# Attention with a soft mixture of experts: second-layer weights in two-row units, weight loads begun later, merged first loads, last group's exponentials by pairs of heads

## The chip, the cores and the metric

One core of one Trainium2 chip runs the kernel. The metric is the device time in microseconds (us). Engines: PE (TensorE), PEld (its weight load), ACT (ScalarE), DVE (VectorE), POOL (GpSimd), SP (SyncE, which here only issues transfers); 16 DMA engines move data between the chip's memory (DRAM here) and the on-chip buffers.

## The reference, cut to what matters

```python
# q, k, v: (8 batches, 12 heads, 448 tokens, 64); cap = 30
s = cap * tanh(q @ k.T / 8 / cap)                 # per batch and head
attn = softmax(s) ; x = attn @ v                  # -> x: 3584 tokens x 768
logits = x @ phi                                  # phi: 768 x 32 (8 experts, 4 slots each)
slot_input = softmax(logits, over tokens).T @ x   # 32 x 768
h = relu(slot_input[e] @ w1[e])                   # w1: 8 x 768 x 1024
slot_out[e] = h @ w2[e]                           # w2: 8 x 1024 x 768
out = softmax(logits, over slots) @ slot_out      # 3584 x 768
```

All inputs and outputs are float32. The kernel computes in bf16 and fp16 with float32 sums.

## The kernel before, in words

**Groups.** The attention is cut into 24 groups of four heads (two pairs of heads, numbered 0 and 1). A group has 14 key tiles (`TILES`, L31): tiles 0 to 6 belong to pair 0, 7 to 13 to pair 1, of 128 keys each; of every seven, one is a "mixed" tile that holds the last 64 keys of both heads. The scores of a group come in six chunks (`CHUNKS`, L34) of 3, 2, 2, 2, 3, 2 tiles: PE computes them (L520, L523), ACT takes the tanh of a chunk at a time out of PSUM (L533). Then ACT takes the exponentials of the first nine tiles in one instruction (L541, 128x9x448). For the other five tiles DVE builds the exponentials as a sum of four terms (L548, `PH` 0 to 3). In the last group these are four tiles, and the fourteenth is a small exponential on ACT of its own (L541, 128x448). PE multiplies by the values (L558): `a0`, `a1` for pair 0; `d` (two tiles), `c0` to `c3` (the four terms) and, in the last group, `e` for pair 1. DVE divides by the sums (L591, L592), PE turns the result (L603), DVE copies it (L607), and the logits and slot sums follow.

**The order of the work.** A planner (`Plan`, from L68) lists all steps of the 24 groups with durations from a table (`COST`, L63) and due times shifted by two more tables (`DUE`, `HOLD`, L50 and L58), and picks the order in which they are written; each step is written by its entry in `EMIT` (L722). Each engine runs its instructions in that order, so a step that waits holds up everything behind it on its engine.

**Transfers.** The POOL queue carries the q loads (L406), the w1 weights in 24 parts of 512 KB (L341) and the w2 weights in 32 parts (L345) of 384 KB, all cast from float32 to bf16 on their way; POOL also casts V (L431). There is no room on chip for all of w2 during the attention: five parts stay in a buffer `w2b`, 27 are written to DRAM as bf16 (`w2d`) and read back by SP at the end (L874, `w2t`). SP issues the K loads (`kraw`, L411; DVE casts them, L417), the V loads (L423, four DMAs a group) and the stores of the output (L945, L963). The planner starts the weight parts at 3000 of its nanoseconds and spreads them up to the end of the attention, with the intervals of w1 and w2 parts as 4 to 3.

**First loads.** `load_first` (L440 to 454) fetches q and k of group 0 as float32: q0, k0 (pair 0), k1, q1 (pair 1), each into a 128x448 piece of `raw`. Each of the four is issued as two DMAs of 64 partitions, 112 KB each; k0 goes by the ACT queue, the rest by SP. Casts (L463), turns (L470) and copies (L477) of pair 0 are written out by hand (L750 to 761); those of pair 1 (`CA`, `T0`, `C0`) are steps of the planner. Memsets of the V buffers follow at L762 to 770.

**The end.** After the last group come the logits, slot sums and the first expert layer (L895), relu (L906, L909), a turn of the hidden values (`h_transp`, L911), and the second layer in two passes (L928): pass 0 gives columns 0 to 383 of the slot outputs, pass 1 columns 384 to 767. Each pass goes through all 64 blocks of 128 hidden units. A w2 part before is four blocks by one half of the columns, so pass 0 reads only half-0 parts; the reads from DRAM (L872) are sorted by half. A cast of half 0 (L985, L986) starts the output products and their stores, which run beside pass 1.

Of the kernel before, what the change touches and what calls it, by code (L numbers as in the profile page):

```python
# [10 lines left out]
BF16 = mybir.dt.bfloat16  # L11
# [6 lines left out]
P = 128  # L18
# [22 lines left out]
ND_LAST = 4  # L41
FULL, ROWS, COLS, QUARTERS = range(4)
# [7 lines left out]
DUE = {"C0k": 58662, "C0q": -424707, "CAk": -62736, "CAq": 128660, "CE": -181216, "CS": 121512, "CW": -420874,  # L50
# [7 lines left out]
HOLD = {"C0k": 102, "C0q": 1186, "CAk": 1500, "CAq": 919, "CE": 125, "CS": 183, "CX": 1447, "Ck": 546, "Cq": 841,  # L58
# [4 lines left out]
COST = dict(quad=9250, lat=200, dma=6000, form=95, sc=100, scm=200, act=0.833, act0=70, ts=242, ts0=90,  # L63
            pvf=31, turn=420, kturn=450, xturn=400, copy=540, kcopy=600, norm=780, vcast=1060, vscale=340, kcast=570, kdiag=300,
            issue=800, load=1400, part1=3200, part2=2450, same=300, page=6000)


class Plan:  # L68
# [5 lines left out]
    def op(self, name, eng, dur, deps=(), due=0.0, take=None, give=None, after=0.0, form=(FULL, FULL), port=False, mm=0):  # L74
        key = name[0] + (str(name[2]) if name[0] in ("PV", "NR", "PH", "EX", "LG", "SS") else "") + \
            (name[1] if name[0] in ("L", "X", "T", "C", "CA", "T0", "C0") else "")
        self.ops[name] = dict(name=name, eng=eng, dur=dur, deps=list(deps), due=due + DUE.get(key, 0.0),
                              key=key, hold=max(0, HOLD.get(key, 0)), take=take, give=give, after=after, form=form, port=port, mm=mm)

    def build(self):  # L80
# [11 lines left out]
        for Q in range(1, NQ):  # L92
            for n, nm in enumerate("kq"):
                t0 = Q * T - (2600, 1800)[n]
                if nm == "k":
                    op(("LK", Q), "SP", 400, [("KC", Q - 2)], t0 - 1.5 * T)
                    op(("XK", Q), "DMV", C["load"], [("LK", Q)], t0 - 1.5 * T)
                    op(("KC", Q), "DVE", C["kcast"], [("XK", Q), ("T", nm, Q - 1)], t0 - 0.5 * T, port=True)
                else:
                    op(("L", nm, Q), "POOL", C["issue"], [("T", nm, Q - 2)], t0 - 1.3 * T)  # L100
                    op(("X", nm, Q), "DMA", C["load"], [("L", nm, Q)], t0 - 1.3 * T)
# [4 lines left out]
        for Q in range(NQ):  # L106
            b, t0, lastq = Q // NQB, Q * T, Q == NQ - 1
            for s in range(nc):
# [21 lines left out]
            op(("EX", Q, 0), "ACT", C["act0"] + C["act"] * S * na, [("TH", Q, sa)],  # L130
               t0 + T * (first[sa] + CHUNKS[sa] + 2.5) / NQT)
            if ne:
                op(("EX", Q, 1), "ACT", C["act0"] + C["act"] * S * ne, [("TH", Q, nc - 1)], t0 + 2 * T)
            for i in range(PH):
# [4 lines left out]
                if i < PH - 1 and k >= 0:  # L139
                    deps.append(("PV", k // (PH - 1), f"c{k % (PH - 1)}"))  # L140
                op(("PH", Q, i), "DVE", C["ts0"] + C["ts"] * ((nd + 1) // 2), deps, t0 + T + 1100 * i, port=True)
            te = t0 + .8 * T
            vs = [("VC", Q), ("VS", Q)]
            op(("PV", Q, "a0"), "PE", 24 * C["pvf"], [("EX", Q, 0)] + vs, te, take=True, mm=24)
            op(("PV", Q, "a1"), "PE", 8 * C["pvf"], [("PV", Q, "a0")], te + 1, mm=8)
            op(("NR", Q, 0), "DVE", C["norm"], [("PV", Q, "a1"), ("SS", (Q - 4) // NQB, 1)], te + 1000,
               give=("PV", Q, "a0"))
            td = t0 + T + 1200
            op(("PV", Q, "d"), "PE", (8 + 4 * (NA - 8)) * C["pvf"], [("EX", Q, 0)] + vs, td - 10, take=True, mm=8 + 4 * (NA - 8))
            for i in range(PH):  # L150
                op(("PV", Q, f"c{i}"), "PE", 4 * nd * C["pvf"],
                   [("PH", Q, i), ("PV", Q, f"c{i - 1}" if i else "d")], td + 1100 * i, mm=4 * nd)
            if ne:
                op(("PV", Q, "e"), "PE", 4 * C["pvf"] * ne, [("EX", Q, 1), ("PV", Q, "c0")], td + 2500, mm=4 * ne)
            op(("NR", Q, 1), "DVE", C["norm"], [("PV", Q, "e"), ("PV", Q, f"c{PH - 1}"), ("SS", (Q - 4) // NQB, 1)],
               td + 5000, give=("PV", Q, "d"))
# [104 lines left out]
def kernel(  # L261
# [62 lines left out]
    w2b = wts.tile([P, KEPT, 4, HD], BF16, name="w2b")  # L324

    blocks = [(i, ft, gg) for i in range(E // 4) for ft in range(NFT) for gg in range(4)]

    def w2_src(n0, n):

        i, ft, gg = blocks[n0]  # L330
        return bass.AP(tensor=moe_w2.tensor,
                       offset=((4 * i + gg) * F + ft * P) * D,
                       ap=[[D, P], [F * D, n], [1, D]])
# [9 lines left out]
    def load_half(dst, n0, half):  # L343
        src = w2_src(n0, 4)
# [720 lines left out]
```

## Time and profile before

| what | value |
|---|---|
| time, median of 3 runs | 292.15 us (292.04 to 292.38) |
| profiled execution's own time | 294.73 us |
| its span, first to last instruction | 292.8 us |
| busy PE / ACT / DVE / POOL | 253.5 / 242.3 / 212.5 / 99.0 us |
| chain that ended last | ACT 38%, PE 31%, DMA 12%, DVE 10% |
| mean granted TensorE clock | 0.938 |
| moved by DMA | 75.30 MB in 59071 packets |

How to read it: the attention fills the span from about 11 to 240 us. ACT works without a break there, apart from the first 48 us, so a wait of ACT inside the attention lengthens the run. Before it come the first loads, behind it the two expert layers and the stores. The profiled execution took 294.73 us, 1.93 more than its span and 2.58 more than the median of the three runs.

### The profile page before, as it was taken

Reading aid. Unit: us, or ns where it says so; the run is one execution under the profiler, and the core shown is the slowest. Engines: PE = TensorE matmul, PEld = TensorE weight load, DVE = VectorE, ACT = ScalarE, POOL = GpSimd, SP = SyncE. Lnnn points to the kernel's source line nnn. Section 1 sums busy time; section 2 is a strip of 40 time slices with the busy share of each in tenths; the row PEclk is TensorE's granted clock in tenths of the full one; section 3 lists DMA queues with packets and bytes.
Section 4 is the critical chain, followed back from the end, with each engine's and each line's share of the span. In section 5 each row is a group of like instructions: output and inputs, shape, how many; then the busy total and the mean of one; then the engine's idle time right before and its main releaser. Section 6 shows DMA issues by size and latency. Waiting matters only on the chain.

```text
span 292.8 us, 10788 instructions
## 1 busy us (share of the span) xinstructions
PE 253.5 (87%) x4697; PEld 177.4 (61%) x4697; DVE 212.5 (73%) x407; ACT 242.3 (83%) x214; POOL 99.0 (34%) x165
## 2 busy tenths in 40 slices
PE   4799949989999999899999989999999879997700
PEld 4366645767766767667767776677676668543300
DVE  2548936878987898798988878987988764248720
ACT  0799957999999999999999999999999981236710
POOL 4463513512462424353446333553335200200000
PEclk9559986999999999999999999999999989999965
DMA  7999999999999999999999999999999999958995
GB/s 136 247 221 253 233 260 257 239 202 199 245 256 229 244 254 250 250 244 244 234 244 249 225 245 226 248 247 228 182 212 319 260 334 405 396 190 328 412 411 227
DMA packets 59071, 75.30 MB, mean 257 GB/s; under 512 B 4880, under 2 KB 48016, under 8 KB 59024
## 3 DMA queue, kind: packets, MB, share of 16 engines
q0 software_dynamic: 30464, 30.50, 63.4%
q1 hardware_dynamic: 28400, 43.89, 45.7%
q8 instruction: 37, 0.61, 0.8%
q10 hardware_dynamic: 160, 0.23, 0.3%
q14 instruction: 10, 0.08, 0.1%
HBM read 94.08 MB, written 21.63 MB: 395 GB/s over the span
## 4 chain that ended last, share of the span: by engine, by line
ACT 38%; PE 31%; DMA 12%; DVE 10%; issue 4%; SPq 1%; DVEq 0%; POOL 0%; ACTq 0%
ACT exa L541 18%; PE pv L558 12%; ACT exd L533 11%; ACT exa L533 8%; PE sc L523 6%; DMA kraw<-in_k_dram 5%; DMA vraw<-in_v_dram 3%; DVE term L548 3%; PE xps L603 2%; DMA raw<-in_q_dram 2%; DMA out_dram<-ob 2%; PE so_ps L928 2%; PE hp L895 2%; PE qps L494 2%; PE sc L520 2%
## 5 line engine op out<-in xcount | busy, mean ns | idle before, releaser
L533 ACT ACTIVATE exa<-sc 128x1344 f16<-128x1344 f32 (+1 forms) x96 | 91.7, 1036 | 5.7 <-PE sc L523 5.3
L541 ACT ACTIVATE exa<-exa 128x4032 bf16<-128x4032 f16 x24 | 86.0, 3585 | 0.0
L548 DVE TENSOR_SCALAR term<-exd 128x2240 uint16<-128x2240 f16 (+1 forms) x72 | 62.6, 892 | 1.6 <-PE pv L558 1.6
L523 PE MATMUL sc<-qT,kT 64*128 64x448 bf16 x288 | 58.0, 372 | 0.8 <-ACT exa L533 0.3
L558 PEld LDWEIGHTS <-term 128*128 128x128 bf16 x1428 | 48.6, 98 | 9.6 <-issue 6.8
L558 PE MATMUL pv<-vb,exa 128*128 128x65 bf16 x1056 | 46.0, 197 | 8.9 <-ACT exa L541 8.1
L558 PEld LDWEIGHTS <-exa 128*128 128x128 bf16 x1056 | 38.6, 100 | 21.7 <-ACT exa L541 10.4
L533 ACT ACTIVATE exd<-sc 128x1344 f16<-128x1344 f32 (+1 forms) x48 | 50.8, 1118 | 0.5 <-DVE xq L592 0.5
L406 POOL DMA_DIRECT2D qb<-in_q_dram x23 | 16.7, 726 | 73.5 <-PE qps L494 60.0
L558 PE MATMUL pv<-vb,term 128*128 128x65 bf16 x952 | 36.8, 195 | 0.0
L592 DVE TENSOR_TENSOR xq<-pv,rec 128x448 bf16<-128x448 f32 (+2 forms) x49 | 30.1, 615 | 3.1
L523 PEld LDWEIGHTS <-kT 64*128 64x128 bf16 x288 | 15.3, 93 | 19.5 <-issue 13.0
L431 POOL CAST vb<-vraw 128x1024 bf16<-128x1024 f32 x24 | 25.5, 1062 | 1.3 <-DMA vraw<-in_v_dram 0.7
L607 DVE COPY xT<-xps 128x896 bf16<-128x896 bf16 x23 | 14.3, 624 | 11.2 <-PE xps L603 11.1
L345 POOL DMA_DIRECT2D w2d<-in_moe_w_dram x27 | 21.1, 799 | 0.8 <-issue 0.8
L548 DVE TENSOR_SCALAR exd<-exd 128x2240 uint16<-128x2240 f16 (+1 forms) x24 | 20.3, 848 | 0.8
L499 DVE COPY kT<-kps 128x1024 bf16<-128x1024 bf16 x23 | 15.8, 688 | 5.1 <-PE kps L490 4.8
L430 POOL COPY seen<-xq 1x1 bf16<-1x1 bf16 x22 | 4.3, 197 | 43.9 <-DVE xq L592 43.9
L558 PE MATMUL pv<-vw,exd 128*128 128x65 bf16 x476 | 18.6, 193 | 0.6
L558 PE MATMUL pv<-vw,term 128*128 128x65 bf16 x476 | 18.6, 193 | 0.3 <-DVE term L548 0.2
L591 DVE RECIPROCAL rec<-pv 128x7 f32<-128x7 f32 (+2 forms) x49 | 9.8, 200 | 11.6 <-PE pv L558 11.6
L520 PE MATMUL sc<-qT,kT 128*128 128x448 bf16 x48 | 17.9, 373 | 0.2 <-ACT exa L533 0.2
(135 smaller groups left out, 315.7 us busy)
## 6 DMA issues: line engine op xcount, KB each, us to landing
w1b<-in_moe_w_dram POOLq DMA_DIRECT2D x24, 512.0 KB, 9.8
w2d<-in_moe_w_dram POOLq DMA_DIRECT2D x27, 384.0 KB, 10.5
w2t<-w2d SPq DMA_DIRECT2D x27, 384.0 KB, 7.7
kraw<-in_k_dram SPq DMA_DIRECT2D x23, 448.0 KB, 7.8
out_dram<-ob SPq DMA_DIRECT2D x9, 768.0 KB, 8.9
vraw<-in_v_dram SPq DMA_DIRECT2D x48, 128.0 KB, 7.1
qb<-in_q_dram POOLq DMA_DIRECT2D x23, 224.0 KB, 7.6
vraw<-in_v_dram SPq DMA_DIRECT2D x48, 96.0 KB, 7.2
```

Of the source, the lines that this page charges most:

```text
L345: pool.dma_start(out=dst, in_=bass.AP(tensor=src.tensor, offset=src.offset + half * HD, ap=[[D, P], [F * D, 4], [1, HD]]))
L406: pool.dma_start(out=t, in_=bass.AP(tensor=srcs[nm].tensor, offset=quad_at(Q), ap=[[NT * DH, P], [2 * S * DH, 2], [1, NT * DH]]))
L431: pool.tensor_copy(vb[Q % 2][:, :, :, 0:DH], vraw[Q % 2])
L499: dve.tensor_copy(new_qkT(nm, Q), ps)
L520: pe.matmul(dst, kT[:, NT - 1:NT + 1, :], qT, start=True, stop=True)
L523: pe.matmul(dst, kT[r, 2 * t:2 * t + 2, :], qT[r], start=True, stop=True)
L533: act.activation(quad_ex(Q, u0, u0 + w).bitcast(F16), ring(Q, s)[:, 0:w, 0:S], ACT.Tanh, scale=qk_scale / cap)
L541: act.activation(t, t.bitcast(F16), ACT.Exp, scale=cap)
L548: dve.tensor_scalar(rows(term_home(Q, i))[:, 0:nd, 0:S].bitcast(U16), quad_ex(Q, NA, NA + nd).bitcast(F16), octaves * 128, base[i], ALU.mu ...
L558: pe.matmul(dst[:, 2 * g + h if g < NF else 2 * g, :], buf[:, q0:q0 + P], vt[:, (SLOTS - 1) * h if a is None else 1 + NF * h + t, :], star ...
L592: dve.tensor_tensor(xq[Q][:, s0:s1, n, :], ps[:, s0:s1, 0:DH], rec.to_broadcast([P, s1 - s0, DH]), op=ALU.mult)
L607: dve.tensor_copy(xTs[Q], held.pop(("x", Q)))
```

## The change

It has four parts.

1. **w2 in two-row units.** A part of w2 is now 256 hidden units by all 768 columns of one expert: a partition takes two neighbouring rows (6144 bytes of float32 in one run) and writes 3072 bytes of bf16. `w2d` tiles are padded to 1664 columns. The hidden units are taken in matching order by `h_transp`, and both passes of the second layer read from the same units, so pass 0 reads all 32.
2. **Planner.** Weight parts begin at 12000 instead of 3000 and their intervals stand as 7 to 5; they are costed at 2800 and 2050 instead of 3200 and 2450. K and q loads of groups 1 to 5 are costed 1200 more. `DUE` and `HOLD` have new numbers, and the last group's steps have keys of their own.
3. **First loads.** Each of q0, k0, k1, q1 is one DMA of 128 partitions instead of two of 64. ACT copies one element (`seen` from `ones`) right behind its issue of k0. The memsets of the V buffers stand ahead of POOL's issues of q1, q2 and phi.
4. **Last group.** The exponentials on ACT are three: tile 13, then tiles 7 and 8, then tiles 0 to 6 (before: tiles 0 to 8, then 13). PE multiplies pair 1 first.

```diff
         def get(eng, nm, n):
-            for h in range(2):
-                eng.dma_start(out=first[nm, n][h * HP:h * HP + HP],
-                              in_=bass.AP(tensor=srcs[nm].tensor, offset=(2 * h + n) * S * DH,
-                                          ap=[[NT * DH, HP], [1, NT * DH]]))
+            eng.dma_start(out=first[nm, n],
+                          in_=bass.AP(tensor=srcs[nm].tensor, offset=n * S * DH,
+                                      ap=[[2 * S * DH, 2], [NT * DH, HP], [1, NT * DH]]))
...
     load_first()
+    act.copy(seen, ones[0:1, 0:1])
     load_k(1)
     load_v(0)
-    load("q", 1)
-    load("q", 2)
-    pool.dma_start(out=phi4[:, :, 0, :], in_=moe_phi.rearrange("(jt ji) s -> ji jt s", ji=P))
...
+    load("q", 1)
+    load("q", 2)
+    pool.dma_start(out=phi4[:, :, 0, :], in_=moe_phi.rearrange("(jt ji) s -> ji jt s", ji=P))
...
-        big = 24
-        total = 4 * big + 3 * (self.parts - big)
+        big, begin = 24, 12000
+        total = 7 * big + 5 * (self.parts - big)
...
-            t = 3000 + (4 * min(k, big) + 3 * max(k - big, 0)) * (NQ - 0.4) * T / total
+            t = begin + (7 * min(k, big) + 5 * max(k - big, 0)) * ((NQ - 0.4) * T + 3000 - begin) / total
...
+    def load_w2(dst, unit):
+        i, fp, gg = unit
+        pool.dma_start(out=dst, in_=bass.AP(tensor=moe_w2.tensor, offset=((4 * i + gg) * F + 2 * P * fp) * D,
+                                            ap=[[2 * D, P], [1, 2 * D]]))
...
-    for n0, half in sorted(w2_spilled, key=lambda x: (x[1], x[0])):
-        t = tl.tile([P, 4, HD], BF16, name=f"w2t{n0}_{half}")
-        sp.dma_start(out=t, in_=w2d[n0, half])
-        w2t[n0, half] = t
+    for unit in w2_spilled:
+        w2t[unit] = tl.tile([P, 2, D], BF16, name="w2t%d_%d_%d" % unit)
+        sp.dma_start(out=w2t[unit].rearrange("p j d -> p (j d)"), in_=w2d[unit][:, 0:2 * D])
...
-            pe.matmul(src[:, ft, :, :], hbs[i][:, ft * P:(ft + 1) * P], own,
+            pe.matmul(src[:, ft, :, :], hbs[i].rearrange("m (t p j) -> m t j p", p=P, j=2)[:, ft // 2, ft % 2, :], own,
...
+            if lastq:
+
+                for i, a, b in ((0, 0, HALF), (2, HALF, NA), (1, NA + nd, NQT)):
+                    op(("EX", Q, i), "ACT", C["act0"] + C["act"] * S * (b - a), [("TH", Q, at[b - 1])],
+                       t0 + 2 * T + 100 * (1 if i == 2 else 2 * i), last=True)
```

What the new tables do is seen in the order of the instructions.

SP, its first instructions, before (the four halves of q0, k1, q1 as pairs; `x2` is two rows alike) and after:

```order
L447 DMA raw_196<-in_q_dram 64x448 x2
L447 DMA raw_196<-in_k_dram 64x448 x2
L447 DMA raw_196<-in_q_dram 64x448 x2
L411 DMA kraw_169<-in_k_dram 128x2x448
L423 DMA vraw_171<-in_v_dram 64x2x256
```

```order
L455 DMA raw_196<-in_q_dram 128x1x448
L455 DMA raw_196<-in_k_dram 128x1x448
L455 DMA raw_196<-in_q_dram 128x1x448
L420 DMA kraw_169<-in_k_dram 128x2x448
L432 DMA vraw_171<-in_v_dram 64x2x256
```

Three issues stand where six stood, ahead of the same loads of K and V.

POOL, the stretch that holds the first w1 parts (`w1b`), the q loads (`qb`) and the V casts (`vb`), before and after:

```order
L341 DMA w1b_87<-in_moe_w_dram 128x2x1024 x2
L406 DMA qb<-in_q_dram 128x2x448 x2
L431 CAST vb_173<-vraw_171 128x16x64
L341 DMA w1b_87<-in_moe_w_dram 128x2x1024
L431 CAST vb_174<-vraw_172 128x16x64
L341 DMA w1b_88<-in_moe_w_dram 128x2x1024
L620 COPY phi_79<-phi_79 128x6x96
L406 DMA qb<-in_q_dram 128x2x448
L341 DMA w1b_88<-in_moe_w_dram 128x2x1024
```

```order
L415 DMA qb<-in_q_dram 128x2x448
L440 CAST vb_173<-vraw_171 128x16x64
L353 DMA w1b_87<-in_moe_w_dram 128x2x1024
L440 CAST vb_174<-vraw_172 128x16x64
L353 DMA w1b_87<-in_moe_w_dram 128x2x1024
L415 DMA qb<-in_q_dram 128x2x448
L353 DMA w1b_87<-in_moe_w_dram 128x2x1024
L415 DMA qb<-in_q_dram 128x2x448
L633 COPY phi_79<-phi_79 128x6x96
```

Two weight parts stood ahead of the first V cast; none stands there now, and they come one at a time between the q loads and casts.

ACT, its last instructions of the attention (`exa` holds tiles 0 to 8, `exd` the others; the 3x448 and 2x448 rows read `sc` and are tanh), before and after:

```order
L533 ACTIVATE exd_165<-sc_191 128x3x448
L533 ACTIVATE exd_165<-sc_192 128x2x448
L541 ACTIVATE exa_163<-exa_163 128x9x448
L541 ACTIVATE exd_165<-exd_165 128x448
```

```order
L541 ACTIVATE exd_165<-sc_191 128x3x448
L541 ACTIVATE exd_165<-sc_192 128x2x448
L552 ACTIVATE exd_165<-exd_165 128x448
L552 ACTIVATE exa_163<-exa_163 128x2x448
L552 ACTIVATE exa_163<-exa_163 128x7x448
```

The small exponential came last and comes first now, and the large one is cut at the border of the two pairs.

More of the change, by code (lines that the diff above doesn't have):

```diff
@@ L148, in build @@
             td = t0 + T + 1200
-            op(("PV", Q, "d"), "PE", (8 + 4 * (NA - 8)) * C["pvf"], [("EX", Q, 0)] + vs, td - 10, take=True, mm=8 + 4 * (NA - 8))
-            for i in range(PH):
+            md = 8 + 4 * (NA - 8)
+            if lastq:
+                op(("PV", Q, "d"), "PE", 4 * nd * C["pvf"], [("PH", Q, 0)] + vs, td, take=True, mm=4 * nd, last=True)
+                op(("PV", Q, "c0"), "PE", md * C["pvf"], [("EX", Q, 2), ("PV", Q, "d")], td + 4000, mm=md, last=True)
+            else:
+                op(("PV", Q, "d"), "PE", md * C["pvf"], [("EX", Q, 0)] + vs, td - 10, take=True, mm=md)
@@ L157, in build @@
+            op(("NR", Q, 1), "DVE", C["norm"], [("PV", Q, "e"), ("PV", Q, "c0"), ("PV", Q, f"c{PH - 1}"), ("SS", (Q - 4) // NQB, 1)],
+               td + 5000, give=("PV", Q, "d"), last=lastq)
             if not lastq:
@@ L323 @@
            for e in range(E - 2)]
-    w2b = wts.tile([P, KEPT, 4, HD], BF16, name="w2b")
+    w2b = wts.tile([P, KEPT, 2, D], BF16, name="w2b")
     blocks = [(i, ft, gg) for i in range(E // 4) for ft in range(NFT) for gg in range(4)]
[L328 to L333, printed above, removed]
+    units = [(i, fp, gg) for i in range(E // 4) for fp in range(NFT // 2) for gg in range(4)]
+    w2_kept, w2_spilled = units[:KEPT], units[KEPT:]
     w1r = moe_w1.rearrange("e (jt ji) f -> ji e jt f", ji=P)
@@ L568, in pv @@
         nd = nd_of(Q)
-        if what == "a0":
+        if what in ("a0", "d") and Q not in normed:
             xq[Q] = normed[Q] = xs.tile([P, NT, 2, DH], BF16, name="xq", tag="xq")
@@ L862 @@
     for a in range(0, P, NS):
-        pe.matmul(junk[a:a + NS, :], ones, w2b[:, 0, 0, :], start=True, stop=True,
+        pe.matmul(junk[a:a + NS, :], ones, w2b[:, 0, 0, 0:HD], start=True, stop=True,
                   skip_group_check=True)
@@ L881, in w2_half @@
     def w2_half(n, half):
-        part = (n - n % 4, half)
-        if part in w2t:
-            return w2t[part][:, n % 4, :]
-        return w2b[:, w2_kept.index(part), n % 4, :]
+        i, ft, gg = blocks[n]
+        unit = (i, ft // 2, gg)
+        t = w2t[unit] if unit in w2t else w2b[:, w2_kept.index(unit), :, :]
+        return t[:, ft % 2, half * HD:(half + 1) * HD]
     hbs = {}
```

84 lines of the change are left out of this document (41 added, 43 removed), and 26 rows, old and new, of tables (DUE, HOLD).

## The prediction

> **What bounds the kernel now.** I began with the stretches of the span, grouped by stage (columns: length, then busy time and count of PE, PEld, DVE, ACT, POOL, then granted clock, DMA share, GB/s).
>
> ```profile
> 0.00:11.23 11.23, 5.79 (x62) 4.35 (x62) 3.31 (x22) 2.73 (x6) 3.70 (x15) 0.83 0.92 178
> ...
> 41.00:48.50 7.50, 5.23 (x52) 3.04 (x53) 5.22 (x10) 2.56 (x3) 2.61 (x4) 0.54 1.12 272
> 48.50:240.10 191.60, 182.11 (x3648) 133.28 (x3644) 161.98 (x301) 190.99 (x158) 75.60 (x112) 1.00 1.17 241
> 240.10:259.40 19.30, 18.79 (x392) 12.65 (x393) 6.29 (x19) 3.69 (x9) 2.36 (x2) 0.93 0.92 357
> 259.40:292.80 33.40, 15.01 (x122) 6.48 (x121) 15.97 (x22) 12.84 (x17) 0.00 (x0) 0.82 0.85 330
> 280.00:288.00 8.00, 0.00 (x0) 0.00 (x0) 0.37 (x1) 0.00 (x0) 0.00 (x0) 0.53 1.01 412
> ```
>
> ACT is busy 190.99 of 191.60 us in the body: nothing that the change does to PE, DVE or the transfers there is worth anything unless it makes ACT idle. What is left to win or lose lies in three places: the first 11.23 us before ACT's first tanh, the hole at 41 to 48.5 us, where ACT has 2.56 busy of 7.50, and the end. The last row, in the output stores, gives what 16 DMA engines reach when they never pause: 412 GB/s, 25.75 GB/s for one.
>
> The start, from the timeline and the rows of the tile `raw`:
>
> ```profile
> 0.74 1.19 ACTq L447 DMA_DIRECT2D raw<-in_k_dram  x2
> 0.74 1.46 SPq L447 DMA_DIRECT2D raw<-in_q_dram  x2
> ...
> 7.24 1.28 ACT L463 ACT_TABLE_LOAD   x1 [7.24 <-DMA raw<-in_q_dram]
> ...
> 8.54 0.66 ACT L463 CAST casts<-raw 128x192 bf16<-128x192 f32 x2
> ...
> 11.23 2.91 ACT L533 ACTIVATE exa<-sc 128x1344 f16<-128x1344 f32 x3 [0.35 <-PE sc L520]
> 11.43 0.40 DVE L463 CAST casts<-raw 128x448 bf16<-128x448 f32 x1 [0.29 <-DMA raw<-in_q_dram]
> 14.43 0.92 ACT L533 ACTIVATE exa<-sc 128x896 f16<-128x896 f32 x1 [0.29 <-PE sc L523]
> ```
> ```profile
> DMA to landing us min/median/max: 2.8/5.7/7.3
> ```
>
> ACT waits 7.24 us for q0, then spends 1.28 on its table before it casts. The last load, q1, is cast by DVE at 11.43, so it landed near 11.14; the tanh chunk that needs pair 1 comes at 14.43, 3.0 us after that cast began.
>
> The hole, from the chain, the timelines of DVE and ACT, and the waits of ACT (total, times, longest):
>
> ```profile
> 27.93 13.86 DMA kraw<-in_k_dram
> ```
> ```profile
> 41.81 0.63 DVE L417 CAST kcast<-kraw 128x896 bf16<-128x896 f32 x1 [4.50 <-DMA kraw<-in_k_dram]
> ```
> ```profile
> 44.72 0.92 ACT L533 ACTIVATE exa<-sc 128x896 f16<-128x896 f32 x1 [3.73 <-PE sc L523]
> 46.35 0.92 ACT L533 ACTIVATE exa<-sc 128x896 f16<-128x896 f32 x1 [0.71 <-PE sc L523]
> 47.77 1.29 ACT L533 ACTIVATE exd<-sc 128x1344 f16<-128x1344 f32 x1 [0.51 <-DVE xq L592]
> ```
> ```profile
> ACT exa L533 <- PE sc L523: 5.3, 4, 3.7
> ```
>
> A K load took 13.86 us and landed at 41.8; its cast could have gone 4.50 us earlier, at 37.3. The scores were late and ACT lost 3.73 + 0.71 + 0.51 = 4.95 us. Of the four waits of the last row, 5.3 in all, two are these, one is the 0.29 at the start, and the fourth is 0.57.
>
> **The change, part by part. First loads.** Each of q0, k0, k1, q1 was two DMAs of 64 rows; it is now one, whose source pattern counts 2 in its outermost dimension, then 64 rows, then 448 numbers, against 128 partitions. No transfer in the profile of before leads with anything but 64 or 128. If a transfer is dealt to the DMA engines along its outermost dimension, 64 or 128 rows make sixteen equal shares, and 2 make two shares. I take this as what happens. The two ends of its price are far apart: on sixteen engines a merged load costs nothing and saves an issue; on two, it goes as follows.
>
> One first load is 2 x 114,688 bytes, so 114.7 kB on each of two engines: 4.45 us at 25.75 GB/s. The fixed part is the quickest landing, 2.8, less 0.3 of moving: 2.5. q0 and k0 are issued together at 0.74 and share the two engines: 0.74 + 2.5 + 2 x 4.45 = 12.1. k1 and q1 follow: 12.1 + 8.9 = 21.0. POOL's q loads of groups 1 and 2 (458.8 kB each at the source, a sixteenth on each engine, 1.1 us) and phi put 2.4 us on the same two engines: q1 lands near 23.4. Pair 0 is no longer the limit: with q0 and k0 at 12 to 13, ACT's first tanh comes near 16 and its three chunks are done near 19. The chunk of pair 1 starts 2.2 to 3.0 us behind q1's cast, at 25.9 to 26.7 instead of 14.43: **+11.5 to +12.3, taken as +12.0**. Down to +10 if POOL's pieces come behind; up to +16.6 if the engines run at the mean of the whole trace:
>
> ```profile
> q1 hardware_dynamic: 28400, 43.89, 45.7%
> ```
>
> 45.7% of 16 x 292.8 us for 43.89 MB is 20.5 GB/s an engine, 5.6 us a load, 4.6 more for four. The early table load (1.28) and POOL's earlier memsets lie in the wait for q0 either way and are worth nothing here.
>
> The Trainium skill has this rule: in "DMA: Bandwidth & Descriptors", section "Why a DMA increments its semaphore by 16 and not by 1", a transfer uses the largest number of engines up to 16 that divides the slowest dimension (other than 1) of both access patterns; for 2 and 128 that is two. No run so far shows a case under 16, so the trace neither bears it out nor contradicts it. The same page, in "Rules for kernel authors", speaks for the merge: two transfers to disjoint partition halves are not worth it, one of 128 partitions is better; by that rule alone the sum would be that of the first rival below.
>
> **Weight loads begun later.** Up to the late K load POOL had issued five weight parts; the first two and the last:
>
> ```profile
> 14.43 1.42 POOL L341 DMA_DIRECT2D w1b<-in_moe_w_dram  x2
> ...
> 30.28 0.72 POOL L341 DMA_DIRECT2D w1b<-in_moe_w_dram  x1
> ```
>
> Each reads 1 MB: 2.5 us at 412 GB/s. The new order puts the first of them behind the first V cast and leaves one or two fewer ahead of the fifth K load, 2.5 to 5 us of traffic less, where 4.5 us was the delay (41.8 against 37.3, where the cast could have gone). And the start, 12 us late, gives the loads that much more time. So the hole goes: −4.95, and 0.3 of the fourth wait of that row, **−5.2**; −3.5 if some 1.5 us of it stays, −5.5 at most. Behind it the body is ACT's again.
>
> **w2 in two-row units.** A part has 128 runs at the source instead of 512.
>
> ```profile
> 60.00:120.00 60.00, 56.77 (x1166) 42.17 (x1167) 50.48 (x96) 59.45 (x48) 21.35 (x34) 1.00 1.10 236
> 140.00:200.00 60.00, 57.96 (x1152) 42.07 (x1152) 51.18 (x97) 60.00 (x53) 27.41 (x40) 1.00 1.24 238
> ```
>
> With w2 in place of w1 the DMA share rises from 1.10 to 1.24 at the same traffic, so the short runs do cost engine time; ACT is busy 60.00 of 60.00 all the same. The work of ACT hides it: 0. If that cover were gone, as it is if loads came late, it would be some 0.5 us a part.
>
> **The end.** Of the last group's exponentials and products:
>
> ```profile
> 236.10 3.57 ACT L541 ACTIVATE exa<-exa 128x4032 bf16<-128x4032 f16 x1
> ...
> 258.26 0.32 ACT L985 CAST so<-so_ps 128x192 bf16<-128x192 f32 x1 [2.67 <-PE so_ps L928]
> ```
> ```profile
> 239.73 2.60 PE L558 MATMUL pv<-vb,exa 128*128 128x65 bf16 x44 [0.78 <-ACT exa L541]
> 242.14 1.50 PE L558 MATMUL pv<-vb,term 128*128 128x65 bf16 x32
> 243.47 0.28 PE L558 MATMUL pv<-vb,exd 128*128 128x65 bf16 x4
> 243.89 0.67 PE L558 MATMUL pv<-vw,term 128*128 128x65 bf16 x16
> ```
> ```profile
> L874 SPq DMA_DIRECT2D w2t<-w2d x27: 319/320/1088, 218.5 to 251.6; - x27
> ...
> DMA to landing us min/median/max: 5.4/7.7/9.4
> ```
>
> Before, PE has 112 products left after the large exponential (44 + 32 + 4 + 16, and 16 more like the last), at 42 to 70 ns; in the new order only pair 0's 32 stand behind the last one. That is 80 fewer, 3.4 to 4.3 us at 42 to 54 ns (the last row, and the first two together), less a last exponential that ends later (three instructions for two, +0.5) and the normalisation that now comes last: some −2.6 for everything up to the second layer. But pass 0 of the second layer now reads all 27 parts that come back from DRAM, where it needed only the half-0 ones. The last is issued at 251.6 and lands at 251.6 + 7.7 = 259.3, later than the cast of half 0 at 258.26. The stream of reads is dense (357 GB/s in that stretch), so I let it come forward by less than the 2.6, to 257.6, and add 0.3 for the last products: cast at 257.9, **−0.3**. The ends: 256.8 (−1.5) if the reads follow the attention closely; 259.6 (+1.3) if they don't move. The stores behind it run at the limit of the engines and shift with it.
>
> **Sum.** Span 292.8 + 12.0 − 5.2 − 0.3 = 299.3; the profiled execution took 294.73, which would give 301.2; against the median of 292.15 it is **298.6 us**. The ends: 292.15 + 10 − 5.5 − 1.5 = 295.2 and 292.15 + 16.6 − 3.5 + 1.3 = 306.5.
>
> **Rivals.**
>
> First, the other side: **the merged loads use all sixteen engines**. For it: a store or a K load of 128 partitions does in before, and the destination here has 128; whoever deals by the destination sees no difference. Against it: the pattern on the source's side leads with 2. Then q0 and k0 land near 4.3 to 5, the table load lies in their wait, and ACT's cast moves from 8.54 to about 5.1: −3.4 (2.9 to 4.0). Time: 292.15 − 3.4 − 5.2 − 0.3 = 283.2. Break-even is where the start costs the 5.5 that the rest brings: q1 landing near 16.6. Two engines are past it (23.4); four would be short of it (half the moving: about 0.74 + 2.5 + 8.9 + 2.4 = 14.5, +3.5, about 290). Chance 0.15; something between, 0.04.
>
> Second: **the hole stays or moves**, since the weight parts that began later come closer to each other (intervals 7 to 5 up to the same end) and meet another K load; the 13.86 us shows how one queue delays another. Against it: the later start leaves the K loads 12 us more, and no wait of ACT for scores after the hole was over 0.57 us in before. Time: 292.15 + 12.0 − 0.3 = 303.9. Chance 0.05.
>
> Third, that **the end's reordering does nothing**, because the weights from DRAM land last: that is already the likeliest in my term (−0.3 instead of −2.6); if they landed early, the forecast would be 296.3, inside the range.
>
> **How the numbers follow.** Forecast 0.76, hole stays 0.05, sixteen engines 0.15, between 0.04. The range of 294 to 306 takes in the first two with the bounds of the start and the end, and leaves out 0.19. A measurement of this kernel can tell about 0.2% (0.6 us) from no change. Slower by more than that: 0.76 + 0.05 + 0.01 of the cases between = 0.82; within it 0.01; faster 0.17.
>
> **What would show it.** In the rows of `raw`: a landing of q0 and k0 at 11 to 13 us and of q1 at 21 to 25 (sixteen engines: all under 8). In ACT's timeline: a first tanh near 16, and a gap of 6 to 8 us ahead of the fourth chunk's tanh near 26. No wait of the K cast for `kraw` over 1 us around 45 to 60, and no gap of ACT there. At the end: fewer than 40 products behind the last exponential, and a cast of half 0 that waits for `so_ps`, with PE waiting for `w2t`. I am wrong as a whole if the first tanh comes before 10 us; the term of the hole is wrong if ACT's waits for `sc` still sum to over 2 us after the fourth chunk.

## The result, and the profile after

The changed kernel takes **311.88 us** (median of 4 runs, 311.15 to 313.64) against 292.1 for the kernel before: a ratio of 1.0686, 95% interval 1.0638 to 1.0734. Slower, as forecast, but 13 us beyond the forecast of 298.6 and outside the range of 294 to 306. The profiled execution took 311.47 us, its span is 309.7. The intervals here and below leave out executions more than 1.5% above the fastest of the same kernel, such as one of 711 us in e8.

The stretches of the changed kernel, cut at its own events (columns as in the prediction: length, busy time of PE, PEld, DVE, ACT, POOL, granted clock, DMA share, GB/s):

```profile
0.00:17.34 17.34, 5.58 (x62) 4.28 (x62) 3.06 (x21) 2.92 (x8) 5.53 (x32) 0.73 0.36 62
17.34:36.00 18.66, 5.41 (x53) 2.27 (x51) 5.78 (x9) 9.40 (x7) 4.21 (x5) 0.50 0.53 133
36.00:44.00 8.00, 7.17 (x74) 4.45 (x74) 4.16 (x8) 3.94 (x5) 0.17 (x1) 0.61 1.02 206
44.00:254.40 210.40, 201.03 (x4078) 147.53 (x4078) 177.36 (x334) 209.97 (x173) 81.26 (x126) 1.00 1.11 248
254.40:274.20 19.80, 15.88 (x312) 9.27 (x310) 4.88 (x15) 2.92 (x7) 2.36 (x2) 1.00 0.90 350
274.20:309.70 35.50, 17.27 (x133) 6.81 (x124) 16.42 (x23) 13.57 (x19) 0.00 (x0) 0.79 0.80 311
```

ACT is busy for 9.40 of 18.66 us behind its first tanh and for 3.94 of the next 8.00, then 209.97 of 210.40. What went wrong lies in the first 44 us and in the end. ACT in the timeline, start and end:

```profile
14.65 0.66 ACT L471 CAST casts<-raw 128x192 bf16<-128x192 f32 x2 [11.27 <-DMA raw<-in_q_dram]
...
17.34 2.10 ACT L541 ACTIVATE exa<-sc 128x1344 f16<-128x1344 f32 x2 [0.35 <-PE sc L528]
28.00 0.92 ACT L541 ACTIVATE exa<-sc 128x896 f16<-128x896 f32 x1 [8.56 <-PE sc L531]
...
38.95 2.10 ACT L541 ACTIVATE exa<-sc 128x1344 f16<-128x1344 f32 x2 [3.49 <-PE sc L528]
42.02 1.85 ACT L541 ACTIVATE exa<-sc 128x896 f16<-128x896 f32 x2 [0.97 <-PE sc L531]
...
250.77 3.64 ACT L552 ACTIVATE exa<-exa 128x896 bf16<-128x896 f16 x2
...
274.25 0.32 ACT L997 CAST so<-so_ps 128x192 bf16<-128x192 f32 x1 [7.13 <-PE so_ps L940]
```

The first cast waits for q0 until 14.65, the fourth chunk of tanh stands at 28.00 instead of 14.43, there is a new gap ahead of group 1 (3.49 and 0.97), none at a K load behind it, and the cast of half 0 waits 7.13 us for the second layer.

The kernel before was profiled a second time, in an execution of 291.48 us, which is nearer to its median than the first (294.73). Its ACT:

```profile
13.32 0.92 ACT L533 ACTIVATE exa<-sc 128x896 f16<-128x896 f32 x1 [0.34 <-PE sc L523]
```
```profile
42.58 0.92 ACT L533 ACTIVATE exa<-sc 128x896 f16<-128x896 f32 x1 [2.69 <-PE sc L523]
44.10 0.92 ACT L533 ACTIVATE exa<-sc 128x896 f16<-128x896 f32 x1 [0.61 <-PE sc L523]
45.52 1.29 ACT L533 ACTIVATE exd<-sc 128x1344 f16<-128x1344 f32 x1 [0.51 <-PE sc L523]
```
```profile
236.65 0.58 ACT L541 ACTIVATE exd<-exd 128x448 bf16<-128x448 f16 x1
...
255.11 0.32 ACT L985 CAST so<-so_ps 128x192 bf16<-128x192 f32 x1 [2.67 <-PE so_ps L928]
```

Its span is 289.7. So the way from one kernel to the other can be cut at the fourth chunk, the last exponential and the cast of half 0 (us; the last exponential ends at 240.14 and 237.23 in the two profiles of before and at 254.41 in the changed kernel):

| stretch | foreseen | after minus before, first profile | after minus before, second profile |
|---|---|---|---|
| start to the tanh of the fourth chunk | +12.0 | +13.6 | +14.7 |
| from there to the end of the last exponential | −4.7 (hole −5.2, cut exponential +0.5) | +0.7 | +2.5 |
| from there to the cast of half 0 | −0.8 | +1.7 | +2.0 |
| cast of half 0 to the end of the span | 0 | +0.9 | +0.9 |
| span | +6.5 | +16.9 | +20.0 |

### The profile page after: what moved, and what is told of

Same layout as the page of the kernel before. It is cut to its first block, busy times and chain, and to the rows that moved or that the text cites. A ratio compares the mean times of both kernels' runs of the same rounds, so it can differ in the third digit from the quotient of the medians.

```text
span 309.7 us, 10803 instructions
## 1 busy us (share of the span) xinstructions
PE 252.3 (81%) x4697; PEld 174.6 (56%) x4697; DVE 211.7 (68%) x407; ACT 242.7 (78%) x216; POOL 93.5 (30%) x165
## 4 chain that ended last, share of the span: by engine, by line
ACT 49%; PE 22%; DMA 19%; DVE 3%; issue 2%; SPq 1%; DVEq 0%; ACTq 0%
ACT exa L552 25%; ACT exd L541 15%; PE pv L569 9%; DMA w2t<-w2d 8%; DMA raw<-in_q_dram 8%; ACT exa L541 7%; PE sc L531 6%; PE xps L616 2%; DMA out_dram<-ob 2%; PE sc L528 2%; PE so_ps L940 1%; ACT eT L650 1%; DMA out_dram<-obh 1%; DVE term L559 1%; PE op L978 1%
## 5 line engine op out<-in xcount | busy, mean ns | idle before, releaser
L552 ACT ACTIVATE exa<-exa 128x4032 bf16<-128x4032 f16 (+2 forms) x25 | 86.1, 3448 | 0.0
L559 DVE TENSOR_SCALAR term<-exd 128x2240 uint16<-128x2240 f16 (+1 forms) x72 | 64.0, 891 | 7.3 <-ACT exd L541 4.1
L569 PEld LDWEIGHTS <-exa 128*128 128x128 bf16 x1056 | 37.9, 99 | 19.1 <-ACT exa L552 10.4
L531 PEld LDWEIGHTS <-kT 64*128 64x128 bf16 x288 | 14.7, 93 | 20.3 <-issue 12.8
L498 PE MATMUL kps<-ident,kcast 128*128 128x128 bf16 x184 | 14.6, 224 | 4.6 <-DVE kcast L426 4.6
L439 POOL COPY seen<-xq 1x1 bf16<-1x1 bf16 x22 | 5.6, 254 | 41.5 <-DVE xq L605 41.5
L353 POOL DMA_DIRECT2D w1b<-in_moe_w_dram x24 | 18.0, 751 | 0.0
L357 POOL DMA_DIRECT2D w2d<-in_moe_w_dram x27 | 16.9, 631 | 1.2 <-issue 1.2
```

The source lines that it names most:

```text
L353: pool.dma_start(out=w1b[e][:, js, :], in_=w1r[:, e, js, :])
L357: pool.dma_start(out=dst, in_=bass.AP(tensor=moe_w2.tensor, offset=((4 * i + gg) * F + 2 * P * fp) * D, ap=[[2 * D, P], [1, 2 * D]]))
L498: pe.transpose(ps[:, :, x, :], src[:, c, :, :].rearrange("p h d -> p (h d)"), ident)
L531: pe.matmul(dst, kT[r, 2 * t:2 * t + 2, :], qT[r], start=True, stop=True)
L552: act.activation(t, t.bitcast(F16), ACT.Exp, scale=cap)
L559: dve.tensor_scalar(rows(term_home(Q, i))[:, 0:nd, 0:S].bitcast(U16), quad_ex(Q, NA, NA + nd).bitcast(F16), octaves * 128, base[i], ALU.mu ...
```

## The experiments

**e0_before: before once more.**

> The kernel before, profiled once more. Its profiled execution took 294.73 us, 2.3 above the median of its runs. Theory A (the hole differs from execution to execution): an execution of 291 to 293 us has ACT gaps at 41 to 48 us of 2 to 3 us in sum instead of 4.95. Rival: the hole is the same 4.95 and something else was long.

Measured: gaps of 2.69 + 0.61 + 0.51 = 3.81 us in an execution of 291.48. The hole does differ between executions, though less than expected; the fourth chunk (13.32 against 14.43) differs as much.

**e1_halves: the first loads alone undone.**

```diff
-            eng.dma_start(out=first[nm, n],
-                          in_=bass.AP(tensor=srcs[nm].tensor, offset=n * S * DH,
-                                      ap=[[2 * S * DH, 2], [NT * DH, HP], [1, NT * DH]]))
+            for h in range(2):
+                eng.dma_start(out=first[nm, n][h * HP:h * HP + HP],
+                              in_=bass.AP(tensor=srcs[nm].tensor, offset=(2 * h + n) * S * DH,
+                                          ap=[[NT * DH, HP], [1, NT * DH]]))
```

> The changed kernel with the first loads again as two DMAs of 64 partitions; all else as changed. Theory A (the merged loads run on two DMA engines and cost the start 13.6 us; a second loss of some 4.5 us is the DVE order, group 0's first term ahead of group 1's K cast; a third of some 2.9 is the end, where pass 0 waits for every w2 read): all raw loads landed before 10 us, fourth tanh chunk at 12 to 14.5 instead of 28.0, a gap of 2 to 4.5 us ahead of group 1's first tanh stays; 295 to 298 us. Rival B (the new order of the attention and the later weights are the larger loss, and the start is hidden in part): 303 to 309 us.

Measured: 292.9 us, ratio to before 0.9985 (0.9949 to 1.0021). **19.0 of the 19.8 us that the change costs are gone when the merged loads alone are undone**, more than either theory gave. ACT begins at 8.05, and the gap ahead of group 1 is smaller but there:

```profile
8.05 2.91 ACT L542 ACTIVATE exa<-sc 128x1344 f16<-128x1344 f32 x3 [0.35 <-PE sc L529]
11.26 0.92 ACT L542 ACTIVATE exa<-sc 128x896 f16<-128x896 f32 x1 [0.30 <-PE sc L532]
```
```profile
19.48 2.10 ACT L542 ACTIVATE exa<-sc 128x1344 f16<-128x1344 f32 x2 [1.86 <-PE sc L529]
22.55 0.92 ACT L542 ACTIVATE exa<-sc 128x896 f16<-128x896 f32 x1 [0.97 <-PE sc L532]
```

28.00 − 11.26 = 16.7 of the 19.0 are the fourth chunk. How few engines the merged loads use is seen in the stretch in which nothing else moves yet; first the changed kernel from 2.5 to 5.5 us, then this one:

```profile
2.50:5.50 3.00, 1.53 (x15) 1.26 (x12) 0.16 (x5) 0.87 (x2) 2.32 (x20) 1.00 0.12 39
```
```profile
2.50:5.50 3.00, 1.53 (x15) 1.27 (x12) 0.29 (x6) 1.08 (x3) 2.31 (x20) 1.00 0.84 228
```

A share of 0.12 of sixteen engines is two (1.9); the halves have 0.84.

**e2_merged_in_before: the merged loads alone, in the kernel before** (the same edit, the other way).

> The kernel before with the merged first loads alone. Theory A: q1 lands near 26 us, fourth tanh chunk near 28; the hole at the fifth K load shrinks or goes, since the loads have 13 us more; no gap ahead of group 1's first tanh over 1.5 us, because there the K cast stands ahead of the term: 301 to 306 us. Rival B: 291 to 295 us.

Measured: 305.68 us, ratio 1.0446 (1.0395 to 1.0496), in the band of theory A.

```profile
31.28 0.92 ACT L532 ACTIVATE exa<-sc 128x896 f16<-128x896 f32 x1 [10.60 <-PE sc L522]
32.62 0.92 ACT L532 ACTIVATE exa<-sc 128x896 f16<-128x896 f32 x1 [0.42 <-PE sc L522]
```

The fourth chunk is 16.9 later than in before's first profile, the time 13.2 us: with the late start no gap follows up to the end of the attention. With before's order the hole goes by the late start alone, and no gap ahead of group 1 comes. So the merged loads cost 13.2 us in the kernel before and 19.0 in the changed one: the parts of the change don't add up. Beside halves the other three parts cost nothing that can be measured (e1); beside merged loads they cost 311.88 − 305.68 = 6.2 us. In the profiles 2.1 of them are there at the end of the last exponential (254.41 against 252.34), 2.8 come between it and the cast of half 0 (19.8 against 17.0 us) and 1.0 behind the cast.

**e7_62_rows: what sets the number of engines.** Each half cut by rows:

```diff
+            for h in range(2):
+                for r0, r1 in ((0, 62), (62, HP)):
+                    eng.dma_start(out=first[nm, n][h * HP + r0:h * HP + r1],
+                                  in_=bass.AP(tensor=srcs[nm].tensor, offset=(2 * h + n) * S * DH + r0 * NT * DH,
+                                              ap=[[NT * DH, r1 - r0], [1, NT * DH]]))
```

> The changed kernel with each first load cut by rows, not merged: 62 + 2 rows of each half. Nothing leads with a literal 2 in the large pieces, but 62 has no divisor up to 16 above 2. If the count of engines is the largest divisor, up to 16, of the leading count: two engines, DMA share near 0.1 and 40 to 52 GB/s from 4 to 20 us, fourth tanh chunk at 24 to 32 us, 306 to 315 us. If only the outer dimension of 2 did it and 62 rows are spread over the engines: first tanh near 8, 291 to 296 us.

Measured: 311.59 us, as the changed kernel and in the band for two engines, the fourth chunk at 28.15, and from 2.5 to 5.5 us:

```profile
2.50:5.50 3.00, 1.53 (x15) 1.26 (x12) 0.16 (x5) 1.40 (x2) 2.31 (x20) 1.00 0.11 42
```

So it is neither the merging nor the literal 2: 62 rows go over two engines, as 62 = 2 x 31 has no larger divisor up to 16, and 64 rows over (nearly) all. That is the rule of the Trainium skill, "DMA: Bandwidth & Descriptors", section "Why a DMA increments its semaphore by 16 and not by 1"; these runs show it for two and for sixteen. The advice of its "Rules for kernel authors", one 128-partition transfer in place of two halves, did not hold for this pattern, which leads with 2 (another row of the same table warns of a small outermost count): following it cost 19.0 us here and 13.2 in the kernel before.

**e3_kcast_first and e5_term_later: the order of DVE.** In the changed kernel DVE takes group 0's first term before it casts K of group 1:

```profile
32.04 2.81 DVE L559 TENSOR_SCALAR term<-exd 128x2240 uint16<-128x2240 f16 x1 [4.10 <-ACT exd L541]
34.77 1.22 DVE L426 CAST kcast<-kraw 128x896 bf16<-128x896 f32 x1
```

That K had landed at 27.55 (SP could issue its load only at 11.24, as the issue of q1 ahead of it took 8.96 us; in before it went at 5.65). Its cast waits behind a term that itself waits for the tanh of group 0's `exd` tiles. The edits, to the changed kernel's order:

```diff
+    order.remove(("KC", 1))                                  # e3
+    order.insert(order.index(("PH", 0, 0)), ("KC", 1))       # e3
+    order.remove(("PH", 0, 0))                               # e5
+    order.insert(order.index(("C", "k", 1)) + 1, ("PH", 0, 0))  # e5
```

> The changed kernel with one step moved: group 1's K cast stands ahead of group 0's first term on DVE; merged loads kept. Theory A: the gaps of 3.49 and 0.97 us ahead of group 1's chunks go, K cast near 28 us instead of 34.8: 306.5 to 308.5 us. Rival C (group 1 is late because its K load landed at 27.5 behind the merged loads, not because of the order): gaps stay, 311 to 312.5 us.

> The changed kernel, merged loads kept, with group 0's first term on DVE moved behind group 1's K cast and behind the copies of its turned q and K (the run with the K cast alone moved ahead left both copies behind the term, and a gap of 1.64 us). Theory A: the gaps of 3.49 and 0.97 us ahead of group 1's chunks go, to under 1 us in all: 306.5 to 309 us. Rival C (group 1 waits for its loads, not for the order): 310 to 312 us.

Measured: e3 310.4 us (ratio to before 1.0612, 1.0553 to 1.067), e5 310.25 (1.0619, 1.0555 to 1.0684). The gaps there fell from 4.46 to 2.57 in e3 and, in e5, to 0.76 + 0.49 + 0.37:

```profile
38.16 0.92 ACT L544 ACTIVATE exa<-sc 128x896 f16<-128x896 f32 x1 [0.76 <-PE sc L534]
39.56 0.92 ACT L544 ACTIVATE exa<-sc 128x896 f16<-128x896 f32 x1 [0.49 <-PE sc L534]
40.85 1.29 ACT L544 ACTIVATE exd<-sc 128x1344 f16<-128x1344 f32 x1 [0.37 <-PE sc L534]
```
```profile
211.64 0.92 ACT L544 ACTIVATE exd<-sc 128x896 f16<-128x896 f32 x1 [2.30 <-PE sc L534]
```

So the order makes most of that gap. The clock is no rival: from 28 to 36 us the granted clock was 0.50 in the changed kernel and 1.00 in e3, e5 and e7, and e7, with the changed kernel's order, has gaps of 3.48 and 0.97 there. But the time came down by some 1.5 us, not by 4.5, and with intervals that overlap: in e5 a gap of 2.30 at 209, whose chain goes back to V loads of 15.24 and 4.66 us, took most of it back (e3 has one of 1.94 there). Theory A had the cause of the gap right and its worth wrong; e5's time lies in rival C's band, e3's in neither.

**e4_halves_kcast: halves, and the K cast ahead.** Both edits from above (e1 and e3).

> Both: first loads as two DMAs of 64 partitions, and group 1's K cast ahead of group 0's first term; all else as changed (late weights, w2 in two-row units, last group by pairs). Theory A: ACT has no gap over 1 us from its first tanh to the end of the attention; the end still waits for the last w2 read, 19 us behind the last exponential: 291 to 294 us. Rival B: 300 or more. Rival D (the late weights bring back a hole of 5 us at some K load once the start is early): 296 to 298.

Measured: 292.49 us, ratio 1.0003 (0.9977 to 1.0028), in the band of theory A. No gap of ACT in the attention is over 0.78 us, and its last exponential ends at 233.27, 4.0 us before that of before's second profile. But nothing of this arrives at the end:

```profile
229.63 3.64 ACT L556 ACTIVATE exa<-exa 128x896 bf16<-128x896 f16 x2
```
```profile
254.76 0.32 ACT L1001 CAST so<-so_ps 128x192 bf16<-128x192 f32 x1 [8.65 <-PE so_ps L944]
```

The cast of half 0 comes 21.5 us behind the last exponential instead of 17.9.

**e13_no_reads: the end without its reads.** To e4:

```diff
-    for unit in w2_spilled:
-        w2t[unit] = tl.tile([P, 2, D], BF16, name="w2t%d_%d_%d" % unit)
-        sp.dma_start(out=w2t[unit].rearrange("p j d -> p (j d)"), in_=w2d[unit][:, 0:2 * D])
...
-        t = w2t[unit] if unit in w2t else w2b[:, w2_kept.index(unit), :, :]
+        t = w2b[:, units.index(unit) % KEPT, :, :]
```

> The kernel with halved first loads and the K cast ahead (292.5 us), without the 27 reads of w2 from DRAM: both passes take the five kept parts in place of the others, so the second layer is not computed with its own weights; as many products as ever. Theory A: no wait of over 3 us for so_ps, cast of half 0 at 15 to 16 us behind the last exponential instead of 21.5, stores begin as much earlier: 283 to 287 us. Rival E' (something else holds the end, say the stores): over 290 us.

Measured: 284.18 us, ratio 0.9718 (0.9684 to 0.9752), 8.3 less than e4.

```profile
248.47 0.32 ACT L996 CAST so<-so_ps 128x192 bf16<-128x192 f32 x1 [2.67 <-PE so_ps L939]
```

The last exponential ends at 233.6 there, so the cast comes 14.9 behind it: the reads cost pass 0 of e4 6.6 us, and the pair-wise exponentials are worth 17.9 − 14.9 = 3.0 where nothing waits for weights (2.6 foreseen). All of the 3.0 lies ahead of the first expert layer, whose products begin 5.9 us behind the last exponential instead of 8.9.

**e6_w2_by_halves, e9_kept_parts_first, e14_kept_last, e12_after_w2_by_halves: which reads pass 0 needs.** e6 puts before's parts (four blocks by one half of the columns, half 0 read back first) into e4. e9 has e5's order in e3's place and issues the five kept parts ahead of the spilled ones; e14 has the same order and keeps the last five parts; e12 is the changed kernel with before's parts.

```diff
-    w2d = {unit: dram.tile([P, 2 * D + P], BF16, name="w2d%d_%d_%d" % unit) for unit in w2_spilled}
+    w2d = {part: dram.tile([P, 4, HD], BF16, name=f"w2d{part[0]}_{part[1]}")
+           for part in w2_spilled}
...
-    for unit in w2_spilled:
+    for n0, half in sorted(w2_spilled, key=lambda x: (x[1], x[0])):
...
-    w2_kept, w2_spilled = w2_parts[:KEPT], w2_parts[KEPT:]
+    w2_kept, w2_spilled = w2_parts[-KEPT:], w2_parts[:-KEPT]
```

(The last two lines are e14's.)

> The kernel with halved first loads and the K cast ahead (292.5 us), with w2 again in parts of four blocks by one half of the columns, half 0 read back first. Theory A (pass 0 waits for the last of 27 reads): the cast of half 0 comes 15 to 17.5 us behind the last exponential instead of 21.5, first stores as much earlier: 287 to 290 us. Rival E (the end is set by the bytes that the DMA engines have to move, reads and stores together): the cast comes earlier but the end does not, 291.5 to 293 us. Rival F (short runs of w2 cost the attention): new gaps of ACT, over 293 us.

> As the kernel with w2 by halves (289.7 us), with the five kept parts issued ahead of the 27 spilled ones, and group 0's first term behind group 1's copies. There the last kept part was issued at 219.85 and landed at 248.51, 28.7 us later, and pass 0, which begins with the kept parts, ended at 252.7. Theory A (pass 0 waits for its weights, whichever come last): cast of half 0 at 15 to 17 us behind the last exponential, no wait of over 4 us for so_ps; 286.5 to 288.7 us. Rival E (the bytes to be moved set the end): cast earlier, time within 0.3% of 289.7.

> As the run with w2 by halves (289.7 us), with the last five parts kept in place of the first five, so that pass 0 needs the parts that land last (28.7 us behind their issue) at its end; group 0's first term behind group 1's copies. Theory A: cast of half 0 at 16 to 17.5 us behind the last exponential, last read of half 1 where it was: 287.5 to 289.5 us. Rival: same as its twin, 289.4 to 290.2 us, since pass 1 waits for the last read either way.

> The changed kernel with one part undone: w2 again in parts of four blocks by one half of the columns. Theory A (in the changed kernel pass 0 waits for all reads, 19.8 us behind the last exponential): cast of half 0 at 15 to 18.5 us behind it, 308 to 310.5 us. Rival E (the bytes set the end): no change, 311 to 312.5 us.

Measured: e6 **289.67 us** (0.9928, 0.9891 to 0.9966), 0.7% faster than the kernel before; e9 292.13 (0.9997, 0.9976 to 1.0017); e14 291.05 (0.9943, 0.9916 to 0.997); e12 310.28 (1.0598, 1.0553 to 1.0644). e6's time is in theory A's band, but not by its path: the cast came 19.3 behind the last exponential, not 15 to 17.5, and PE waited for a kept part, whose load is one of POOL's last:

```profile
219.85 28.66 DMA w2b<-in_moe_w_dram
```

In e12 that took 30.46 us, and its cast came 21.2 behind: undoing this part alone moved the wait to another weight, so its time, in theory A's band too, doesn't bear the theory out. With two-row units, at the same place in POOL's order, the slowest kept part took 14.0 us (e4). In e9 and e14 the cast came at 15.5 and 15.8, as theory A had it (for e14 a little early). Yet e9 is slower than e6, and e14 can't be told from it; neither time lies in the band of either theory. Pass 1 took over the wait for the last read. e9, then e14:

```profile
250.17 0.32 ACT L1009 CAST so<-so_ps 128x192 bf16<-128x192 f32 x1 [2.67 <-PE so_ps L952]
...
262.73 0.58 ACT L994 ACTIVATE obh<-op,winv 128x384 f32<-128x384 f32 x1 [8.33 <-PE op L990]
```
```profile
249.47 0.32 ACT L1009 CAST so<-so_ps 128x192 bf16<-128x192 f32 x1 [2.67 <-PE so_ps L952]
...
261.09 0.58 ACT L994 ACTIVATE obh<-op,winv 128x384 f32<-128x384 f32 x1 [6.55 <-PE op L990]
```

So "an earlier cast of half 0 is an earlier end" fell: the end also waits for the last read, and in that rival E was right.

**e8_late_weights_in_before, e11_two_weights_earlier, e10_early_start_in_before: the hole.** e8 issues before's first 17 weight parts two places later in POOL's order; e11 takes e9 and issues the first twelve two places earlier; e10 gives before the early copy on ACT and the memsets ahead of POOL's first issues.

```diff
+    put = {vc: [ws[0], ws[1]]}                  # e11: two parts ahead of the first V cast
+    for i in range(0, 10):                      # e11
+        put.setdefault(at[i], []).append(ws[i + 2])
...
+    act.copy(seen, ones[0:1, 0:1])              # e10
```

> The kernel before with its first 17 weight parts issued two places later in POOL's order (the first one where the third stood), nothing else changed. Theory A (weight parts crowd the fifth K load): no ACT gap over 1 us at 41 to 48 us, attention 2.5 to 5 us shorter; since before its end had to wait for computation, not reads, most of it arrives: 288 to 290.5 us. Rival G (the K load is late for another reason): gap stays, 292 to 293 us.

> As the run with the kept parts first, with the first twelve weight parts two places earlier in POOL's order, so that two stand ahead of the first V cast as in before. Theory A (the later weights took the hole away): gaps of 2 to 5 us ahead of group 3 to 5's chunks, 1 to 3 us slower than its twin. Rival G (the hole was not the weights' doing): within 0.3% of its twin.

> The kernel before with two things of the changed start, the early copy on ACT (its table loads while the first loads travel) and the memsets ahead of POOL's first issues; first loads in halves, order and weights as before. Theory A (the start is worth 3.2 us, but K loads in the first 45 us are bound by what the DMA engines move, so that the hole takes some of it back): first tanh near 8.05 instead of 11.23, gaps at 35 to 48 us of 5 us or more in sum, 290.5 to 292 us. Rival H (nothing is taken back): 288.3 to 289.5 us.

Measured: e11 295.59 us against its twin's 292.13, 3.5 us more where 1 to 3 were expected, and the hole is back:

```profile
44.08 0.92 ACT L566 ACTIVATE exa<-sc 128x896 f16<-128x896 f32 x1 [4.98 <-PE sc L556]
45.71 0.92 ACT L566 ACTIVATE exa<-sc 128x896 f16<-128x896 f32 x1 [0.71 <-PE sc L556]
```

e8 gained nothing: 292.27 (1.0017, 0.9984 to 1.005). In its profile, of a long execution (295.24 us), the hole shrank to gaps of 1.02, 0.71, 0.51 and 0.41 us at 40 to 46, but a new one came late in the attention, behind a q load that POOL's queue took 15.65 us to land:

```profile
140.76 0.92 ACT L552 ACTIVATE exa<-sc 128x896 f16<-128x896 f32 x1 [4.31 <-PE sc L542]
```

So early weights can make the hole, and issuing them later in before's order shrinks it without shortening the run. Whether the other executions of e8 have that new gap, and what else the new order does at the hole (the K and q loads stand elsewhere too), is open. e10: 292.24 (1.0022, 0.9989 to 1.0054). The fourth chunk came at 11.20, 2.1 earlier than in before's second profile, and the gaps behind it added up to 6.1 instead of 3.8:

```profile
23.91 0.92 ACT L533 ACTIVATE exa<-sc 128x896 f16<-128x896 f32 x1 [4.01 <-PE sc L523]
```

All of it was given back, as theory A had it, but at 18 to 27 us more than at 35 to 48: the 4.01 stand behind a K load that took 11.75 us.

## Why the prediction was wrong, point by point

The direction was right; the size was not. Against the second profile of before the span grew by 20.0 us where 6.5 were foreseen. Of the 13.5 us between them 2.7 lie in the start, 7.2 in the stretch with the hole, 2.8 between the last exponential and the cast of half 0, and 0.9 behind that. The step that failed most is the hole, −5.2: no gap was expected behind the fourth chunk, and the new order of DVE made one.

- **First loads, +12.0: right in mechanism, undersized.** Two engines it is (share 0.12; e7). Against the second profile of before the term is 14.7. The forecast took 25.75 GB/s for an engine; from 2.5 to 5.5 us two engines moved 39 GB/s, 19.5 each, near the prediction's other end, 20.5. With it q0 and k0 come out at 0.74 + 2.5 + 2 x 5.6 = 14.4, and ACT's cast began at 14.65. The slip was to take the rate of dense output stores for these loads; why an engine moves less here (the rows are 1792 bytes) no run separates.
- **The table load and the memsets, nothing: right here**, as they lie in the wait for q0. Beside halves they are worth 2 to 3 us: they bring the first tanh from 11.23 and 10.07 in before's two profiles to 8.05 in e1 and 8.00 in e10.
- **The hole, −5.2: right in the place, wrong in the sum.** The old hole went (no gap over 0.4 us behind 44 us). But the forecast left out a step: it did not look at what stands ahead of group 1's K cast on DVE. The new order puts a term there, and 3.49 + 0.97 = 4.46 us of gap came back at once, over the 2 us that the prediction had named as the sign of this term being wrong. Also, the 4.95 was that of a long execution; the second has 3.81. And the hole's going was not worth its length: e4, without a gap over 0.78 us, has this stretch 1.8 us shorter than before's second profile, not 4.7. With merged loads and before's order (e2) the stretch is 5.4 us shorter than in the changed kernel; yet moving the cast or the term alone (e3, e5) brought only some 1.5 us of the run, so how much of the 7.2 is this one step's doing stays in part open.
- **w2 in two-row units hidden in the attention: not contradicted.** ACT was busy 209.97 of 210.40 us. Their price is at the end: with before's parts again e6 has a ratio of 0.9928 where e4 has 1.0003. In the changed kernel the same step (e12 against it) is not clear of the noise.
- **The end, −0.3: the failed assumption is the 1.7 us by which the last read was to come forward.** The mechanism was named (pass 0 now needs all 27 reads), but the last read is issued at 266.0, 11.6 us behind the last exponential, where before had 251.63 − 240.14 = 11.5. The reads don't follow the shorter chain of PE: from 260 to 266 us they run at 397 GB/s with a DMA share of 1.03, close to the 412 of the stores, and the last of them are issued only when earlier ones have landed. The chain that ended last goes through three reads in a row:

```profile
L887 SPq DMA_DIRECT2D w2t<-w2d x27: 319/320/1078, 233.2 to 266.0; - x27
```
```profile
248.69 9.20 DMA w2t<-w2d
257.99 7.95 DMA w2t<-w2d
266.00 7.68 DMA w2t<-w2d
273.72 0.50 PE so_ps L940 x5
```

  The cast came 19.8 behind the last exponential instead of 18.1; foreseen was 17.3. In before PE waits for no read in pass 0.

- **The reference.** The sum was made on a profiled execution of 294.73 us and carried over to the median of 292.15 as if all its stretches shrank alike; the 2.6 us between them sit in the start and the hole, terms that the change replaces. That alone is some 3 us of the miss: against the first profile the span missed by 10.4, against the second by 13.5.
- **Rivals.** The sixteen engines were wrong; their time of 283.2 was too. e1 is that case, at 292.9: the start's gain came nearly as foreseen (the first tanh 3.2 us earlier than in before's first profile and 2.0 than in the second; foreseen 3.4), and was lost at group 1's gap and at the end, where the cast of half 0 came at 255.84 against 255.11 in before's second profile.

Left open: why a term takes 2.81 us at 32.04 and 0.85 at 38.06 (POOL issued loads and cast V beside the first), and which of POOL's transfers makes which V or K load late in a given execution.

## What to carry to other kernels

Look at the leading count of both sides of every DMA pattern, and at the DMA share while it runs alone: a share of 0.12 says two engines. When a table moves an order, read on each engine what now stands ahead of the step that the bound engine needs next. And where a shorter stage doesn't shorten the run, find the transfer that the next stage waits for: here 4 to 7 us of a shorter attention were worth nothing until the reads of the weights changed.

## What the runs showed of the hardware that was not expected

- The last part that stays on chip, loaded by POOL's queue while SP's queue sends a dense stream of reads, took 28.66 and 30.46 us to land in e6 and e12. As a two-row unit at the same place (e4, changed kernel) the slowest took 14.0 and 13.9, and in before's two profiles, with e6's form of part but another order, 10.8 and 13.4. So neither the stream nor the form alone makes it slow; what in the order does is open.
- 62 rows moved as slowly as a merged transfer of 128 (42 and 39 GB/s); halves of 64 rows gave 228.
- The late K load took 13.86 and 13.93 us in the two profiled executions of the kernel before, but the gaps of ACT there were 4.95 and 3.81 us.
- Issuing the last merged load took SP 8.96 us; in before the issues of its two halves took 2.06 together.
